# GpSimd tasks of an SSM-plus-SwiGLU kernel wait by semaphore for VectorE's groups of SBUF operations

## The chip, the core and the metric

The kernel runs as one program on 1 core of one Trainium2 chip. The metric is the device time of that core in microseconds. Three runs of the kernel before gave 634.55, 634.59 and 632.18 us, median 634.55 us. Lower is better. The engines are called as the profile calls them: PE is TensorE's matmul, PEld its weight load, DVE is VectorE, ACT is ScalarE, POOL is GpSimd and SP is SyncE, which issues every DMA of this kernel.

## What is computed

The input `x` has 2048 rows of 512 columns. Its rows are normalized, and the result goes down two branches, which are multiplied at the end:

```python
xn = _layernorm(x, axis=-1)
s = _A_ref(xn, A_re, A_im, B_re, B_im, C_re, C_im, log_dt, Dskip)
g = _silu(_B_ref(xn, w_gate, w_up, w_down))
return x + s * g
```

Branch A is a diagonal state-space model. For each of the 512 channels a kernel `K[l] = Re(sum_n C_n * exp(dt*A_n*l) * dt*B_n)` over 128 states is built for 2048 positions, and `xn` is convolved with it by FFTs of length 4096; `xn * Dskip` is added. Branch B is a SwiGLU layer: `(silu(xn @ w_gate) * (xn @ w_up)) @ w_down` with an inner width of 1792.

## The kernel before

**The work.** Branch B is done in float16 pairs: each operand is split into a high and a low half, and three products replace one float32 product. `x` is cut into 8 blocks of 256 rows (index b), the inner width into 7 chunks of 256 columns (index c). A unit (b, c) is 24 matmuls for the gate and 24 for the up side (L708), a silu on ACT (L729), a product on DVE (L731), a cast to the high half on ACT (L733), the low half on DVE (L734), and, some units later, 6 matmuls into the output for each half block (L750). Before that each weight chunk is scaled and split: for `w_up` chunks 1 to 6 POOL multiplies by the scale (L674), ACT casts (L675) and POOL subtracts (L676); for all others ACT scales (L678) and DVE subtracts (L679).

Branch A has four stages. First the parameters are turned into phases and logarithms: DVE does long chains of 128x256 operations whose inputs and outputs all lie in SBUF (L823 to L963: groups of 1 to 11 instructions), with some products on POOL (L821). This is done twice, for two halves of the channels. Second, tables of angles and amplitudes are made on POOL: eight batches of small operations (L1020 to L1061), and from each batch four angle tables (L1079) and four amplitude tables (L1087). For each table ACT takes cosine and sine (L1102 to L1104), DVE multiplies by the amplitudes (L1122 to L1130) and PE multiplies and sums (L1151, 32 small float32 matmuls). Third come the transforms (L572, L1184, L1236, L1243, L1283), with products on DVE (L1261, L1263) and sums on POOL (L1265, L1266). Last, `final` forms the output (L1330 on PE, L1339 on DVE, L1342 on POOL).

**What sets the order.** All this work is entered as tasks in a plan (class `Plan`). A task has an engine, an estimated duration, the buffers it reads and writes, and a due time from the table `W`. `Plan.run` is a list scheduler: it walks through time, starts on each free engine the ready task with the earliest due time, and returns the tasks sorted by their planned start. The program is then written out in that order, one task after the other, so each engine executes its instructions in the planned order, and the tile framework puts semaphore waits where data or a buffer demands them. Planned times have no other effect on the chip: an engine goes on as soon as the data is there. `keep_warm` fills planned gaps of PE with matmuls whose result nobody reads (L1430).

**The port in the plan.** A task can carry the mark `port`. Every POOL task has it, and of the DVE tasks those that were entered with `port=True`: the reciprocal square roots of the layer norm (L535 to L540), the normalization of the rows (L547), the low halves of weights (L679), the scales of `w_down` (L653 to L660), all groups of the parameter stage (L823 to L963 and the exponentials L935 to L952) and the addition of `Dskip` (L1196). In the plan two port tasks never overlap: `start_one` starts each one no earlier than the end of the last:

```python
t.start = max(now, port_free) if t.port else now
...
if t.port:
    port_free = t.end
```

In the program nothing of this is left before the change: if DVE falls behind its planned time, a POOL task that was planned behind a DVE group may run beside it. DVE tasks that take an input from PSUM (L731, L734, L1122 to L1130, L1261, L1263, L1339) do not carry the mark, nor do some very small ones on SBUF (L633).

All working buffers lie in one SBUF tile, `arena`, so most names in the profile read `arena`; the line tells what an instruction is.

Of the kernel before, what the change touches and what calls it, by code (L numbers as in the profile page):

```python
# [46 lines left out]
     "c_akb": 16, "c_gj": 10, "c_kr": 25, "c_y": 42, "c_y2": 16, "c_bh": 6, "c_bt": 14, "c_fx": 15, "c_fz": 2,  # L47
     "c_ot": 24, "c_hh": 15, "c_a": 34, "ah": 384.828, "rs": 4.584, "n1": 14}
REUSE = 0.25
WARM_FROM, WARM_SPAN, WARM_IDLE, WARM_SHARE, WARM_DUR = 1.5, 3.4, 1.0, 0.8, 0.213  # L50
MAGIC = 12582912.0
TWO32 = 4294967296.0
# [23 lines left out]


class Task:
    __slots__ = ("eng", "dur", "fn", "pr", "due", "root", "seq", "deps", "succ", "bufs", "wait", "ready", "dma", "port", "f32", "slack", "ahead", "start", "end")


class Plan:
# [19 lines left out]
    def add(self, eng, dur, fn, rd=(), wr=(), up=(), pr=0.0, c=5, dma=0.0, root=False, port=None, f32=False, slack=0.0, ahead=None):  # L102

        t = Task()
        t.eng, t.dur, t.fn, t.pr, t.due, t.root, t.seq, t.dma = eng, dur, fn, (c, pr), pr, root, len(self.tasks), dma
        t.f32, t.slack, t.ahead = f32, slack, W["ah"] if ahead is None else ahead  # L110
        t.port = eng == "POOL" if port is None else port
        deps = set()
        for b in rd:
            deps.update(b.full)
            deps.update(b.part)
        for b in up:
            deps.update(b.full)
            deps.update(b.reads)
        for b in wr:
            deps.update(b.full)  # L120
            deps.update(b.part)
            deps.update(b.reads)
        for b in rd:
            b.reads.append(t)
        for b in up:
            b.part.append(t)
        for b in wr:
            b.full.append(t)
        t.bufs = list(dict.fromkeys(b for b in (*rd, *wr, *up) if b.kind))
        for b in t.bufs:  # L130
            b.left += 1
        t.deps = deps
        t.succ = []
        self.tasks.append(t)
        return t

    def run(self):
# [14 lines left out]
        ends = []  # L152
        leaving = []
        order = []
# [91 lines left out]
        while left:  # L246
            while leaving and leaving[0][0] <= now + 1e-9:
                give(heapq.heappop(leaving)[3])
            while ends and ends[0][0] <= now + 1e-9:
                _, _, t = heapq.heappop(ends)  # L250
                for b in t.bufs:
                    b.left -= 1
                    if not b.left:
                        heapq.heappush(leaving, (t.end + REUSE, t.seq, b.name, b))
                for s in t.succ:
# [5 lines left out]
            for e in engs:  # L261
                q, h = later[e], heaps[e]
                while q and q[0][0] <= now + 1e-9:
                    _, seq, t = heapq.heappop(q)
# [18 lines left out]
                raise RuntimeError(f"the plan is stuck at {now}: {stuck}, room {room}, banks {banks}")  # L283
            now = min(nxt)
        self.span = max(t.end for t in order)
        order = self.keep_warm(order)
        self.place([b for b in dict.fromkeys(b for t in order for b in t.bufs) if b.kind == "sb"])
        return order

    def keep_warm(self, order):  # L290

        pe = [t for t in order if t.eng == "PE"]
        held = {}
        for t in order:
            for b in t.bufs:
                if b.kind != "sb":
                    o = held.setdefault(b, [t.start, t.end])
                    o[1] = max(o[1], t.end + REUSE)  # L300
        gaps, at = [], WARM_FROM
        for t in pe:
            if t.start - at > 0.3:
                gaps.append((at, t.start))
            at = max(at, t.start + t.dur)
        idle = lambda a: sum(max(0.0, min(e, a + WARM_SPAN) - max(s, a)) for s, e in gaps)
        more = []
        for s, e in gaps:
            if max(idle(a) for a in (s, s - WARM_SPAN / 2, e - WARM_SPAN)) < WARM_IDLE:
                continue  # L310
            free = [(k, i) for k in "ts" for i in range(self.BANKS[k])
                    if not any(b.at == (k, i) and o[0] < e + 0.3 and o[1] > s - 0.3 for b, o in held.items())]
            n = int((e - s - 0.2) * WARM_SHARE / WARM_DUR)
            if n < 1 or not free:
                continue
            for i in range(n):
                t = Task()
                t.eng, t.start, t.dur, t.bufs, t.fn = "PE", s + i * WARM_DUR, WARM_DUR, [], self.warm(free[-1])
                t.end, t.dma, t.deps, t.port, t.f32 = t.start + t.dur, 0.0, set(), False, False
                more.append(t)  # L320
        self.warmed = len(more)
        return sorted(order + more, key=lambda t: t.start)
# [102 lines left out]
def kernel(  # L425
# [7 lines left out]
    nc = tc.nc  # L433
# [45 lines left out]
    bufs = []  # L479
# [18 lines left out]
    def load(dst, src, names, size, pieces, pr, rd=(), ahead=None):  # L498
        add("SP", 0.15, lambda: sy.dma_start(dst(), src), up=names, rd=rd, pr=pr, dma=dma_us(size, pieces), root=True, ahead=ahead)  # L499


    def c_load(name, t, src, pr):
        load(lambda: t, src, [key(name)], 65536, 128, pr)

    add("DVE", 0.2, lambda: (V.memset(ones, 2.0 ** -26), V.memset(halfpi, math.pi / 2)), up=[key("ones")], c=0)
    add("POOL", 0.6, lambda: G.memset(dsk, 0.0), wr=[key("dsk")], c=0)


# [174 lines left out]
    seq = [(b, c) for c in range(NC) for b in range(FB)] + [(b, c) for b in range(FB, NB) for c in range(NC)]  # L683
# [750 lines left out]
    order = pl.run()  # L1434
    for b in bufs:
        b.t = arena if b.kind == "sb" else bank_t[b.at[0]][b.at[1]]
    for t in order:
        t.fn()


# [27 lines left out]
```

## Time and profile before

| | |
|---|---|
| runs of the kernel before | 634.55, 634.59, 632.18 us |
| the profiled execution's own time | 634.03 us |
| span of its profile | 632.3 us |
| mean granted clock of PE over the span | 0.985 |
| PE busy | 606.7 us (96%) |
| DVE busy | 473.3 us (75%) |
| ACT busy | 333.9 us (53%) |
| POOL busy | 331.9 us (52%) |

The span goes from the first instruction to the last; the execution's own time holds 1.7 us more around it. PE is nearly always busy, so what can be gained or lost on it is its idle time and the stretches in which its clock is granted only in part. The stages differ much: DVE is busy 48.6 of the 50 us from 50 to 100 us and 47.5 of the 50 us from 150 to 200 us, but 21.1 of the 50 us from 550 to 600 us. So engines are read in the stage in question and in order of time. In a row of the timeline stand the start in the span, the duration, the engine, the line, the operation, what it writes and reads, the shapes, how many instructions are merged, and in brackets the idle time before it with what ended it.

### The profile page before, as it was taken

How to read it: one execution, taken by the hardware profiler on the slowest of the kernel's cores; microseconds unless marked ns; L12 is line 12 of the kernel's file. 1: busy time of each engine (PE TensorE's matmuls, PEld its weight loads, DVE VectorE, ACT ScalarE, POOL GpSimd, SP SyncE). 2: the span in 40 equal slices, each digit the busy share in tenths (PEclk: the TensorE clock that was granted, in tenths of full speed). 3: DMA queues.
4: the chain of work that ended last, by engine and by line, in shares of the span. 5: the costliest groups of instructions: out<-in, count | busy, mean ns of one | idle time of the engine just before them, and what ended most of it. 6: DMA issues, size and time to landing. Idle time of an engine off the chain costs nothing.

```text
span 632.3 us, 18214 instructions
## 1 busy us (share of the span) xinstructions
PE 606.7 (96%) x7545; PEld 414.8 (66%) x7545; DVE 473.3 (75%) x970; ACT 333.9 (53%) x665; POOL 331.9 (52%) x301
## 2 busy tenths in 40 slices
PE   7989999999979999999999999999999999999894
PEld 3768787576656767776766766766567766557641
DVE  5999999867999897989876967967756566645124
ACT  4977567275635547674877675755642233221100
POOL 0254412798654557767788687976506042431012
PEclk9999999999998999999999999999999999999998
DMA  9985223134000525232313434490396898998997
GB/s 247 356 271 154 81 68 101 35 109 144 18 1 34 108 62 102 92 111 51 82 72 75 116 106 85 69 298 2 118 245 137 279 371 263 257 251 225 227 253 214
DMA packets 134210, 93.06 MB, mean 147 GB/s; under 512 B 72176, under 2 KB 117488, under 8 KB 134128
## 3 DMA queue, kind: packets, MB, share of 16 engines
q1 hardware_dynamic: 134128, 91.90, 52.4%
q8 instruction: 59, 0.97, 0.7%
q14 instruction: 23, 0.19, 0.1%
HBM read 58.98 MB, written 32.90 MB: 145 GB/s over the span
## 4 chain that ended last, share of the span: by engine, by line
PE 44%; DMA 2%; issue 2%; ACT 1%; SPq 1%; DVE 1%; POOL 0%; POOLq 0%; DVEq 0%; ACTq 0%
PE gu L708 20%; PE z L750 10%; PE s L1151 3%; PE s L1236 3%; PE s L1243 2%; PE s L1330 2%; DMA arena<-bs_d 2%; PE s L1283 1%; PE s L1184 1%; PE s L572 1%; DMA out_dram<-arena 1%; DVE arena L1339 0%; SPq L1315 0%; SPq L499 0%; PE t L1283 0%
## 5 line engine op out<-in xcount | busy, mean ns | idle before, releaser
L708 PE MATMUL gu<-arena,wg 128*128 128x256 f16 x1344 | 157.9, 274 | 4.5 <-ACT arena L729 3.8
L750 PE MATMUL z<-wd,arena 128*128 128x512 f16 x672 | 158.6, 380 | 2.0 <-DVE arena L734 1.9
L708 PEld LDWEIGHTS <-wu 128*128 128x128 f16 x1344 | 131.2, 99 | 31.0 <-issue 10.0
L708 PEld LDWEIGHTS <-wg 128*128 128x128 f16 x1344 | 130.9, 98 | 29.2 <-issue 8.4
L708 PE MATMUL gu<-arena,wu 128*128 128x256 f16 x1224 | 144.4, 276 | 5.5 <-DVE arena L734 4.3
L750 PEld LDWEIGHTS <-arena 128*128 128x128 f16 x672 | 61.2, 98 | 82.5 <-issue 14.3
L1087 POOL TENSOR_TENSOR arena<-arena 128x1536 f32<-128x1536 f32 x32 | 91.1, 2851 | 44.5 <-PE s L1151 21.2
L1079 POOL TENSOR_TENSOR arena<-arena 128x1024 int32<-128x1024 int32 x32 | 63.1, 1971 | 27.2 <-ACT t L1104 10.1
L729 ACT ACTIVATE arena<-gu,inv 128x512 f32<-128x512 f32 x56 | 38.5, 687 | 59.4 <-PE gu L708 53.3
L733 ACT CAST arena<-gu 128x512 f16<-128x512 f32 x51 | 29.9, 587 | 64.8 <-DVE gu L731 63.6
L731 DVE SCALAR_TENSOR_TENSOR gu<-gu,shc,arena 128x512 f32<-128x512 f32 x51 | 38.5, 754 | 32.7 <-PE gu L708 32.6
L1102 ACT ACTIVATE t<-arena 128x512 f32<-128x512 int32 x64 | 38.8, 606 | 37.7 <-DVE arena L1124 36.2
L1265 POOL TENSOR_TENSOR arena<-arena 128x512 f32<-128x512 f32 x16 | 20.4, 1275 | 69.3 <-DVE arena L1263 30.7
L1122 DVE TENSOR_TENSOR arena<-arena,t 128x512 f32<-128x512 f32 x64 | 43.6, 681 | 15.6 <-ACT t L1103 7.6
L1342 POOL TENSOR_TENSOR arena<-arena 128x512 f32<-128x512 f32 x12 | 15.2, 1268 | 57.9 <-DVE arena L1339 34.0
L1151 PEld LDWEIGHTS s<-arena 128*32 128x32 f32 x2048 | 31.4, 109 | 19.4 <-issue 13.9
L1103 ACT ACTIVATE t<-t,halfpi 128x512 f32<-128x512 f32 x64 | 42.5, 664 | 1.8
L1104 ACT ACTIVATE t<-arena 128x512 f32<-128x512 int32 x64 | 38.5, 602 | 6.2 <-DVE arena L1263 3.5
L1151 PE MATMUL s<-arena 128*32 128x64 f32 x2048 | 41.3, 222 | 0.0
L734 DVE TENSOR_TENSOR arena<-gu,arena 128x512 f16<-128x512 f32 x51 | 34.8, 682 | 7.2 <-ACT arena L733 7.0
L1339 DVE TENSOR_TENSOR arena<-s,arena 128x512 f32<-128x512 f32 (+1 forms) x20 | 11.3, 581 | 25.6 <-DMA out_dram<-arena 11.7
L1128 DVE SCALAR_TENSOR_TENSOR arena<-arena,t 128x256 f32<-128x256 f32 x64 | 26.4, 412 | 4.1 <-ACT t L1104 4.1
(205 smaller groups left out, 945.3 us busy)
## 6 DMA issues: line engine op xcount, KB each, us to landing
arena<-in_A_u_dram SPq DMA_DIRECT2D x64, 128.0 KB, 3.9
ax_d<-arena SPq DMA_DIRECT2D x32, 256.0 KB, 2.3
ak_d<-arena SPq DMA_DIRECT2D x16, 512.0 KB, 7.4
arena<-ak_d SPq DMA_DIRECT2D x16, 512.0 KB, 7.0
arena<-ax_d SPq DMA_DIRECT2D x16, 512.0 KB, 6.5
bs_d<-arena SPq DMA_DIRECT2D x32, 256.0 KB, 5.1
arena<-in_B_w_down_dram SPq DMA_DIRECT2D x14, 512.0 KB, 5.3
arena<-bs_d SPq DMA_DIRECT2D x14, 512.0 KB, 6.9
```

The costliest lines, as they stand in the source:

```text
L708: T.matmul(pg.t[:, i * 256:(i + 1) * 256].rearrange("p (a t) -> p a t", a=2), w[:, wl, d, i * P:(i + 1) * P], x[:, :, xl, d, :], start=(k ...
L729: add("ACT", 0.69, lambda: S.activation(sg.f32(), pg.t, AF.Silu, scale=inv[:, c, 0:1]), rd=[pg], wr=[sg], c=1, pr=e)
L731: add("DVE", 0.75, lambda: V.scalar_tensor_tensor(pu.t, pu.t, shc[:, c:c + 1], sg.f32(), op0=ALU.mult, op1=ALU.mult), rd=[sg], wr=[pu], c= ...
L734: add("DVE", 0.7, lambda: V.tensor_tensor(hh.view(F16)[:, 512:1024], pu.t, hh.view(F16)[:, 0:512], op=ALU.subtract), rd=[pu], wr=[hh], c=1 ...
L750: T.matmul(z.t, h[:, hl, i * 256 + t * P:i * 256 + (t + 1) * P], w[:, wl, i], start=(c == 0 and i == 0 and k == 0), stop=(c == NC - 1 and ...
L1079: G.tensor_tensor(a, h_[:, :, :, None].to_broadcast([P, 2 * GT, 4, 8]), l_[:, :, None, :].to_broadcast([P, 2 * GT, 4, 8]), op=ALU.add)
L1087: G.tensor_tensor(e, p_[:, :, :, None].to_broadcast([P, 3 * GT, 4, 8]), q_[:, :, None, :].to_broadcast([P, 3 * GT, 4, 8]), op=ALU.mult)
L1102: add("ACT", 0.62, lambda: S.activation(tc_.t, a(), AF.Abs, scale=SIN_SCALE), rd=[an], wr=[tc_], pr=pr)
L1103: add("ACT", 0.7, lambda: S.activation(tc_.t, tc_.t, AF.Sin, bias=halfpi, scale=-1.0), rd=[key("ones")], wr=[tc_], c=4, pr=pr)
L1104: add("ACT", 0.62, lambda: S.activation(ts.t, a(), AF.Sin, scale=SIN_SCALE), rd=[an], wr=[ts], pr=pr + 0.2)
L1122: V.tensor_tensor(o[:, :, 0:64].rearrange("p d (s j) -> p d s j", s=2), e[:, :, 0:64].rearrange("p d (s j) -> p d s j", s=2), t[:, :, None ...
L1151: T.matmul(kt[h * 32:(h + 1) * 32, (r * GD + dd) // 4], o[:, ri, dd + h, 64:96], o[:, ri, dd + h, 0:64], start=(ri == 0), stop=(ri == 1), ...
```

## The change

After the order is fixed, a new pass, `part_ports`, goes through it. For each POOL task it looks at the last DVE port task ahead of it in the order. If that DVE task was planned to start less than 8 us earlier, and no POOL task has been tied to it yet, the POOL task is tied to it. When the program is written, the first instruction of the tied POOL task gets a dependency on the last instruction of the DVE task, which becomes a semaphore wait on POOL. 50 of the 190 POOL tasks are tied. The plan, its order, the buffers and the durations stay as they are. DVE gets no wait for POOL.

```diff
+APART = 8.0
...
     def part_ports(self, order):
+        last = told = None
+        for t in order:
+            if t.port and t.eng == "DVE":
+                last = t
+            elif t.port and t.eng == "POOL" and last is not None and last is not told and t.start - last.start < APART:
+                t.after = told = last
...
         self.span = max(t.end for t in order)
+        self.part_ports(order)
         order = self.keep_warm(order)
...
+    def made():
+        return nc.m.functions[-1].blocks[-1].instructions
+
+    ends = {}
     for t in order:
+        n = len(made())
         t.fn()
+        new = made()[n:]
+        ends[t] = new[-1]
+        if t.after is not None:
+            tc.add_manual_dep(new[0], ends[t.after].name, mybir.DependencyInfo(mybir.DependencyClass.Sync, mybir.DependencyReason.DATA),
+                              reason="ports apart")
```

The instructions of PE, DVE, ACT and SP stand in the same order with the same counts as before; on POOL the order is the same too, and 12 more semaphore instructions stand in it. What differs is what POOL's instructions wait for. In the new file these lines have numbers that are higher by 15 (L821 is L836, L1079 is L1094, L1087 is L1102).

The first place is POOL's part of the early weight stage, from about 28 to 55 us. Before:

```order
L676 TENSOR_TENSOR wu<-wd,wu 128x1024 [waits Activation_49]
L674 TENSOR_TENSOR wd<-wd,scw 128x1024 [waits DMAHW6_49,DVE_49]
L821 TENSOR_TENSOR arena<-arena 128x256 [waits DMAHW7_49,DMAHW4_49]
L821 TENSOR_TENSOR arena<-arena 128x256 [waits DMAHW5_49]
L821 TENSOR_TENSOR arena<-arena 128x256 [waits DMAHW2_49,Pool_49]
```

The same five instructions with the change:

```order
L691 TENSOR_TENSOR wu<-wd,wu 128x1024 [waits DVE_49,Activation_49]
L689 TENSOR_TENSOR wd<-wd,scw 128x1024 [waits DMAHW6_49,DVE_49]
L836 TENSOR_TENSOR arena<-arena 128x256 [waits DMAHW7_49,DMAHW4_49,DVE_49]
L836 TENSOR_TENSOR arena<-arena 128x256 [waits DMAHW5_49]
L836 TENSOR_TENSOR arena<-arena 128x256 [waits DMAHW2_49,Pool_49]
```

The subtraction (L676) gets a wait for DVE's L679, the first product (L821) one for the next L679. The multiplication between them (L674) waited for DVE before too, for its scale; now it waits for a later instruction of DVE, the end of the group L842 to L846.

The second place is POOL's table stage from about 165 to 203 us. Before:

```order
L1087 TENSOR_TENSOR arena<-arena 128x1536 [waits DVE_49,PE_49,Pool_49]
L1079 TENSOR_TENSOR arena<-arena 128x1024 [waits Activation_49]
L821 TENSOR_TENSOR arena<-arena 128x256 [waits DMAHW4_49,DMAHW2_49,Pool_49]
L821 TENSOR_TENSOR arena<-arena 128x256
L821 TENSOR_TENSOR arena<-arena 128x256 [waits Pool_49]
L1087 TENSOR_TENSOR arena<-arena 128x1536 [waits DVE_49,PE_49]
L1079 TENSOR_TENSOR arena<-arena 128x1024
L821 TENSOR_TENSOR arena<-arena 128x256 [waits Pool_49]
L1087 TENSOR_TENSOR arena<-arena 128x1536 [waits DVE_49]
L1079 TENSOR_TENSOR arena<-arena 128x1024 [waits Activation_49]
```

With the change:

```order
L1102 TENSOR_TENSOR arena<-arena 128x1536 [waits PE_49,Pool_49]
L1094 TENSOR_TENSOR arena<-arena 128x1024 [waits DVE_49,Activation_49]
L836 TENSOR_TENSOR arena<-arena 128x256 [waits DMAHW4_49,DMAHW2_49,Pool_49]
L836 TENSOR_TENSOR arena<-arena 128x256
L836 TENSOR_TENSOR arena<-arena 128x256 [waits DVE_49,Pool_49]
L1102 TENSOR_TENSOR arena<-arena 128x1536 [waits PE_49]
L1094 TENSOR_TENSOR arena<-arena 128x1024 [waits DVE_49]
L836 TENSOR_TENSOR arena<-arena 128x256 [waits Pool_49]
L1102 TENSOR_TENSOR arena<-arena 128x1536 [waits DVE_49]
L1094 TENSOR_TENSOR arena<-arena 128x1024 [waits DVE_49,Activation_49]
```

The first amplitude table (L1087) is not tied. The angle table behind it waits for DVE's L825, the third of the three products (L821) for the end of DVE's group L842 to L846, the next angle table (L1079) for the end of the group that begins with L838 and L839 and holds L851 and L852, the last amplitude table for the end of the group L858 to L863, and the last angle table for the end of L935 to L939. The amplitude table in the middle is not tied either; it stands behind the third product. Where a wait for DVE is gone (the first and the middle amplitude table), an earlier wait of POOL on the same semaphore already covers it.

More of the change, by code (lines that the diff above doesn't have):

```diff
@@ L78 @@
 class Task:
-    __slots__ = ("eng", "dur", "fn", "pr", "due", "root", "seq", "deps", "succ", "bufs", "wait", "ready", "dma", "port", "f32", "slack", "ahead", "start", "end")
+    __slots__ = ("eng", "dur", "fn", "pr", "due", "root", "seq", "deps", "succ", "bufs", "wait", "ready", "dma", "port", "f32", "slack", "ahead", "start", "end", "after")
 class Plan:
@@ L109, in add @@
         t.eng, t.dur, t.fn, t.pr, t.due, t.root, t.seq, t.dma = eng, dur, fn, (c, pr), pr, root, len(self.tasks), dma
+        t.after = None
         t.f32, t.slack, t.ahead = f32, slack, W["ah"] if ahead is None else ahead
@@ L288, in run, with part_ports @@
         return order
+    def part_ports(self, order):
+        last = told = None
[4 more added lines that the diff above has]
+                t.after = told = last
     def keep_warm(self, order):
@@ L318, in keep_warm @@
                 t.eng, t.start, t.dur, t.bufs, t.fn = "PE", s + i * WARM_DUR, WARM_DUR, [], self.warm(free[-1])
+                t.after = None
                 t.end, t.dma, t.deps, t.port, t.f32 = t.start + t.dur, 0.0, set(), False, False
```

## Prediction

> **What bounds the kernel now.** I read the page's busy times first, then PE's list of waits, then the timelines of PE, DVE and POOL around the two longest waits.
>
> ```profile
> span 632.3 us, 18214 instructions
> PE 606.7 (96%) x7545; PEld 414.8 (66%) x7545; DVE 473.3 (75%) x970; ACT 333.9 (53%) x665; POOL 331.9 (52%) x301
> PE gu L708 <- ACT arena L729: 4.4, 4, 2.9
> PE gu L708 <- DVE arena L734: 4.3, 1, 4.3
> ```
>
> PE bounds the kernel: it idles 632.3 - 606.7 = 25.6 us. Whatever the change does to POOL and DVE counts only where it moves PE's idle time. The last two rows (waits: total, times, longest) name the largest: one wait of 4.3 us for DVE's L734, and one of 2.9 us for ACT's L729. Here is the first of them, on PE:
>
> ```profile
> 181.49 2.76 PE L750 MATMUL z<-wd,arena 128*128 128x512 f16 x12
> 188.53 5.28 PE L708 MATMUL gu<-arena,wu 128*128 128x256 f16 x24 [4.28 <-DVE arena L734]
> 178.19 2.78 PE L708 MATMUL gu<-arena,wg 128*128 128x256 f16 x24
> 188.50:195.40 6.90, 6.87 (x62) 4.60 (x62) 6.73 (x15) 2.79 (x6) 1.96 (x1) 0.62 0.10 38
> ```
>
> PE is ready at 181.49 + 2.76 = 184.25 and starts at 188.53. After that the same 24 matmuls take 5.28 instead of 2.78 us, and the window from 188.5 to 195.4 has a granted clock of 0.62 (the column behind the five engines). So this stall costs 4.28 + 2.50 = 6.8 us. Why L734 is late stands in DVE's rows, and POOL's beside them:
>
> ```profile
> 166.26 2.04 DVE L825 TENSOR_SCALAR arena<-arena 128x256 f32<-128x256 f32 x1
> 172.79 2.94 DVE L845 TENSOR_TENSOR arena<-arena 128x256 f32<-128x256 f32 x1
> 175.77 1.93 DVE L846 TENSOR_SCALAR arena<-arena 128x256 f32<-128x256 f32 x1
> 180.71 2.89 DVE L839 TENSOR_TENSOR arena<-arena 128x256 f32<-128x256 f32 x1
> 184.55 0.29 DVE L838 TENSOR_SCALAR arena<-arena 128x256 f32<-128x256 f32 x1
> 184.87 0.43 DVE L839 TENSOR_TENSOR arena<-arena 128x256 f32<-128x256 f32 x1
> 187.80 0.68 DVE L734 TENSOR_TENSOR arena<-gu,arena 128x512 f16<-128x512 f32 x1
> 165.32 2.84 POOL L1087 TENSOR_TENSOR arena<-arena 128x1536 f32<-128x1536 f32 x1 [4.87 <-PE s L1151]
> 172.44 3.01 POOL L1087 TENSOR_TENSOR arena<-arena 128x1536 f32<-128x1536 f32 x1
> 175.42 2.13 POOL L1079 TENSOR_TENSOR arena<-arena 128x1024 int32<-128x1024 int32 x1
> 180.48 2.84 POOL L1087 TENSOR_TENSOR arena<-arena 128x1536 f32<-128x1536 f32 x1 [2.19 <-DVE arena L1130]
> ```
>
> The same L839 takes 2.89 us at 180.71 and 0.43 at 184.87. The long one ends at 183.60, just behind the POOL table that ends at 180.48 + 2.84 = 183.32; the next one meets no POOL instruction. L845 ends at 175.73, L1087 at 175.45; L846 at 177.70, L1079 at 177.55. So a DVE instruction on SBUF alone that starts beside a running POOL instruction ends with it, while POOL loses at most 0.17 us (3.01 against 2.84). DVE pays, and the change makes POOL wait.
>
> **The change at this stall.** Free lengths are 0.43 us for a two-input operation and 0.29 for a TENSOR_SCALAR (rows above). The L1087 at 172.44 and the L1079 behind it now run after L846, since the L821 ahead of them is tied to it: L845 and L846 shrink by 2.94 - 0.43 + 1.93 - 0.29 = 4.15 us. The L1087 at 180.48 now waits for the group L858 to L863, so L839 no longer meets it: 2.89 - 0.43 = 2.46 us more. Against that the first L1087 slides: it starts behind L846's new end (177.70 - 4.15 = 173.55) and one L821 (the three at 40.89, below, take 2.63 us together, so 0.9), so it runs from 174.4 to 177.2, and L839 now comes at 180.71 - 4.15 = 176.56: 0.6 us of the 2.46 are lost to it. L734 is then earlier by 4.15 + 2.46 - 0.6 = 6.0 us and ends at 182.5, ahead of PE's 184.25. Even with nothing gained at L839, it ends at 188.48 - 4.15 = 184.33, and the stall is 0.1 us. **I take the whole 6.8 us**; the low end, if the two tables merely meet other instructions of the same groups, is nothing. L825 at 166.26 stays long: the L1087 that it meets is not tied.
>
> **The stall at 46.6 us.**
>
> ```profile
> 40.94 2.78 PE L708 MATMUL gu<-arena,wu 128*128 128x256 f16 x24
> 46.63 4.45 PE L708 MATMUL gu<-arena,wg 128*128 128x256 f16 x24 [2.91 <-ACT arena L729]
> 37.03 2.14 DVE L842 TENSOR_SCALAR arena<-arena 128x256 f32<-128x256 f32 x1
> 39.21 2.00 DVE L843 TENSOR_TENSOR arena<-arena 128x256 f32<-128x256 f32 x1
> 42.97 0.70 DVE L846 TENSOR_SCALAR arena<-arena 128x256 f32<-128x256 f32 x1
> 43.59 0.74 DVE L731 SCALAR_TENSOR_TENSOR z<-z,shc,arena 128x512 f32<-128x512 f32 x1
> 38.98 1.94 POOL L674 TENSOR_TENSOR wd<-wd,scw 128x1024 f32<-128x1024 f32 x1
> 40.89 2.63 POOL L821 TENSOR_TENSOR arena<-arena 128x256 f32<-128x256 f32 x3
> ```
>
> The group L842 to L846 lasts from 37.03 to 43.67, and L731 stands behind it; L731 releases ACT, and ACT releases PE. With L674 held until the group ends, L843 to L846 need 3 x 0.43 + 0.29 and some 0.03 us between them, 1.7 us, from 39.21, so the group ends at 40.9, 2.8 us earlier, which covers the 2.91 us but for 0.1. The matmuls lose 4.45 - 2.78 = 1.67 us to the clock, so this stall costs 4.6 us. How much of it reaches the end is another matter, because later a chain of its own comes in:
>
> ```profile
> 110.67 1.15 ACT L678 ACTIVATE wd<-arena,scw 128x1024 f16<-128x1024 f32 x1
> 113.45 1.41 DVE L679 SCALAR_TENSOR_TENSOR wd<-arena,scw,wd 128x1024 f16<-128x1024 f32 x1
> 115.31 1.46 PE L750 MATMUL z<-wd,arena 128*128 128x512 f16 x6
> 70.62 0.16 PE L624 MATMUL s<-hsq,ones 128*128 128x2 bf16 x1 [0.79 <-DVE hsq L623]
> 79.61 2.78 PE L708 MATMUL gu<-arena,wg 128*128 128x256 f16 x24 [0.92 <-ACT arena L729]
> ```
>
> The last chunk of `w_down` is cast until 111.82, its low half is ready at 114.86, and PE uses it at 115.31, with filler matmuls just ahead. If PE comes there 4.6 us earlier, it waits for this chain. DVE's L679 can follow ACT 113.45 - 111.82 = 1.6 us sooner, no more, unless ACT and the load come sooner too. So the gain here lies between 0 and 4.6 us, or 6.3 with the two small waits at 70.62 and 79.61 us, in a stretch in which DVE is as late. **I take 1.5 us**, by this 1.6.
>
> **What the waits cost.** Behind a waiting POOL instruction stand the tables, and for those wait ACT's L1102, DVE's L1122 and, through them, PE's L1151. The tightest place I found:
>
> ```profile
> 221.57 2.11 POOL L1079 TENSOR_TENSOR arena<-arena 128x1024 int32<-128x1024 int32 x1 [7.14 <-DVE arena L946]
> 227.56 1.75 DVE L883 RECIPROCAL arena<-arena 128x256 f32<-128x256 f32 x1
> 228.98 0.62 ACT L1102 ACTIVATE t<-arena 128x512 f32<-128x512 int32 x1
> 229.63 0.66 ACT L1103 ACTIVATE t<-t,halfpi 128x512 f32<-128x512 f32 x1
> 233.58 0.69 DVE L1122 TENSOR_TENSOR arena<-arena,t 128x512 f32<-128x512 f32 x1 [0.88 <-PE s L803]
> ```
>
> This angle table is tied to the group that ends with L883 at 229.31. It then ends at 231.4 instead of 223.68, and ACT's L1102 starts 2.4 us late. Its cosine follows 1.3 us after its start (L1103 ends at 230.29), at 232.7, still ahead of DVE's 233.58. So DVE covers it; uncovered it would be 2.4 us. The other end is nothing. I take 0.5 us. 12 more semaphore instructions on POOL stand on no path to PE.
>
> **Sum.** 632.3 - 6.8 - 1.5 + 0.5 = 624.5 us of span. Around the span lie 634.03 - 632.3 = 1.7 us: 626.2 us for the profiled execution, which was 0.5 us below the median of the runs. So **626.7 us** for the median, 1.2% less.
>
> TensorE: Matmul & The Clock Gate, section Part 1: The HAM clock gate, of the Trainium skill, says that the clock falls to half after an idle window of about 3.4 us. The 4.28 us stall fits this; the 2.91 us stall with its 4.45 us matmuls is shorter than that and lost clock all the same. By that rule the early stall would be priced at 2.9 instead of 4.6 us, and the sum would stay as it is, since only 1.5 of it is counted.
>
> **Rivals.** *A rest of the clash stays.* POOL is ordered behind DVE, but DVE is not ordered behind POOL: the untied L1087 slides by 2 us, as worked out above, and may meet more of the next group. For it speaks L825 (166.26), which stays long. If half of the 4.28 us remains as a stall with clock loss in proportion, the first term is 3.4 us instead of 6.8: 626.7 + 3.4 = 630.1 us. Against it: L734 has 1.8 us to spare by the working. The Trainium skill (SBUF — State Buffer, section Who interferes with whom) says that whichever of the two starts first holds the shared ports for its whole instruction and the other blocks; that is this rival's mechanism, and the rows of L839 agree as far as POOL comes first.
>
> *The gain goes into a later limit.* The end is dense with transfers:
>
> ```profile
> 608.00:616.00 8.00, 7.59 (x39) 3.52 (x40) 0.00 (x0) 0.26 (x1) 0.00 (x0) 1.00 1.06 244
> 440.00:448.00 8.00, 8.00 (x91) 6.02 (x89) 6.20 (x14) 4.70 (x8) 8.00 (x6) 1.00 0.01 2
> SPq L1199 <- DVE arena L1196: 15.9, 2, 10.4
> ```
>
> From 608 to 616 us the transfers' share (the last column but one) is over 1 and DVE does nothing. If this were a bound of its own, little would be gained: 633.5 us. Against it: from 440 to 448 us the share is 0.01, and the transfers behind that wait for DVE's L1196 (10.4 us at a time), so their start moves with the compute.
>
> *Slower: the tables come late.* If DVE's groups do not get shorter, each tied POOL task waits out its group in full. The place is the table at 221.57: it comes 2.4 us too late for ACT. ACT executes in order, so the silu and the cast for PE stand behind; PE stalls 2.4 us, and at the ratio of the early stall (1.67 / 2.91) loses 1.4 us of clock. With both old stalls left this is 634.55 + 3.8 = 638.4 us. It decides from the point where a table's delay exceeds its reader's reserve: here 7.7 against 228.98 - 223.68 = 5.3 us. Against it: L839's two lengths.
>
> *The waits do nothing,* because DVE is done before POOL comes: 634.5 us. Against it, the rows of 180.48 and 38.98: the one starts before the group L858 to L863, which stands behind L734 at 187.80, the other before L846's end at 43.67.
>
> **How the numbers follow.** Forecast 0.60, rest of the clash 0.18, later limit 0.10, tables late 0.07, waits without effect 0.05. About 0.5% is what a measurement of this kernel can tell: below 631.4 us is faster, above 637.7 slower. Forecast and first rival are faster: 0.78. Later limit and no effect are the same: 0.15. Tables late: 0.07. Downwards the range reaches the whole early gain, 6.3 instead of 1.5 us: 626.7 - 4.8 = 621.9. Upwards it takes in the first rival and stops at 633.0, ahead of the later limit; what is left out is about 0.2.
>
> **What would show it.** Right: no PE wait above 1 us between 50 and 590 us, a granted clock of 1.0 around 185 us; L845, L846 and L839 in this stage below 1.2 us; L825 still near 2; the L1087 after the L821 starting behind L846; PE's L750 on the last `w_down` chunk still at 112 to 115 us. Wrong: PE waiting for L1151's inputs or for ACT's L729 between 215 and 300 us, L1102 waiting for POOL's L1079 there, or DVE's groups as long as before.

## The result and the profile after

The changed kernel takes 618.92 us (median of four runs, 618.50 to 620.62) against 634.57 us for the kernel before, timed beside it: the ratio is 0.976, with a 95% interval of 0.972 to 0.980. A second series gave 619.64 us and 0.979 (0.976 to 0.982). The change gains 2.1 to 2.4%, between 13 and 16 us. The forecast was 626.7 us with a range from 621.9 to 633.0 us: right in its sign, but only about half of the gain, and the time lies 3 us below the range.

The page of the changed kernel and PE's list of waits there (total, times, longest). In it L708 is L723, L734 is L749, L750 is L765 and L839 is L854.

```profile
span 616.7 us, 18226 instructions
PE 599.4 (97%) x7545; PEld 411.9 (67%) x7545; DVE 444.4 (72%) x970; ACT 335.0 (54%) x665; POOL 327.9 (53%) x301
PE z L765 <- DVE arena L749: 2.1, 1, 2.1
PE gu L723 <- ACT arena L744: 0.5, 2, 0.3
```

DVE is busy 28.9 us less with the same 970 instructions, POOL 4.0 us less. PE idles 17.3 us in place of 25.6, and it is busy 7.3 us less, 4.2 of which are the lost clock behind the two stalls (1.67 + 2.50). Both waits that bounded the kernel before are gone: L723 now waits 0.5 us in all for ACT's silu (L744), and no longer at all for DVE's L749.

PE's timeline in the changed kernel around the two places and near the end (start and duration of the groups of matmuls), then the row of the kernel before that answers to the last one, and the changed kernel's window from 184 to 191 us, in which the column behind the five engines is the granted clock:

```profile
39.98 2.78 PE L723 MATMUL gu<-arena,wu 128*128 128x256 f16 x24
42.65 2.78 PE L723 MATMUL gu<-arena,wg 128*128 128x256 f16 x24
...
174.51 2.76 PE L765 MATMUL z<-wd,arena 128*128 128x512 f16 x12
177.11 2.78 PE L723 MATMUL gu<-arena,wu 128*128 128x256 f16 x24
...
577.90 0.59 PE L765 MATMUL z<-wd,arena 128*128 128x512 f16 x2
```

```profile
593.07 0.59 PE L750 MATMUL z<-wd,arena 128*128 128x512 f16 x2
```

```profile
184.00:191.00 7.00, 7.00 (x99) 4.85 (x104) 6.32 (x18) 5.43 (x16) 1.92 (x2) 1.00 0.10 37
```

Neither group waits, and both run at full clock. The same instructions in the two kernels give **PE's lead**, the measure used from here on. At the 24 matmuls of 39.98 us it is 40.94 - 39.98 = 0.96 us. This part is not the change's: ahead of the first clash the lead differs from trace to trace, from -0.9 to +1.9 us in the kernels below, so each lead is read together with its start. At the 12 matmuls ahead of the late stall it is 181.49 - 174.51 = 6.98 us, so the early part gave 6.0 us. At the next 24 matmuls it is 188.53 - 177.11 = 11.42, and as they take 2.78 in place of 5.28 us, 13.92 behind them: the late stall gave 6.9 us. Near 578 us, at the two L750 that start at 593.07 us in the kernel before, it is 15.17.

DVE's and POOL's timelines at the late stall, changed kernel:

```profile
159.28 2.05 DVE L840 TENSOR_SCALAR arena<-arena 128x256 f32<-128x256 f32 x1
165.63 0.42 DVE L860 TENSOR_TENSOR arena<-arena 128x256 f32<-128x256 f32 x1
166.09 0.29 DVE L861 TENSOR_SCALAR arena<-arena 128x256 f32<-128x256 f32 x1
169.01 1.20 DVE L853 TENSOR_SCALAR arena<-arena 128x256 f32<-128x256 f32 x1
170.31 0.43 DVE L854 TENSOR_TENSOR arena<-arena 128x256 f32<-128x256 f32 x1
174.94 0.68 DVE L749 TENSOR_TENSOR arena<-gu,arena 128x512 f16<-128x512 f32 x1
166.53 0.73 POOL L836 TENSOR_TENSOR arena<-arena 128x256 f32<-128x256 f32 x1 [1.68 <-DVE arena L861]
```

L860 and L861 (L845 and L846 before) fell from 2.94 and 1.93 to 0.42 and 0.29 us; the tied L836, with the tables queued behind it, waits for L861. L840, which meets an untied table, still takes 2.05 us.

### The profile page after: what moved, and what is told of

The parts are those of the page before. It is cut to its first block, busy times and chain, and to the rows that moved or that the text cites. A ratio compares the mean times of both kernels' runs of the same rounds, so it can differ in the third digit from the quotient of the medians.

```text
span 616.7 us, 18226 instructions
## 1 busy us (share of the span) xinstructions
PE 599.4 (97%) x7545; PEld 411.9 (67%) x7545; DVE 444.4 (72%) x970; ACT 335.0 (54%) x665; POOL 327.9 (53%) x301
## 4 chain that ended last, share of the span: by engine, by line
PE 85%; DMA 6%; DVE 4%; SPq 2%; ACT 2%; issue 1%; DVEq 0%
PE gu L723 41%; PE z L765 21%; PE s L1166 6%; DMA arena<-bs_d 3%; PE s L1251 3%; PE s L587 2%; DMA arena<-zg_d 2%; PE s L1258 2%; PE z L723 2%; PE s L1345 2%; PE s L1298 1%; PE s L1199 1%; DMA arena<-in_A_u_dram 1%; PE s L570 1%; SPq L530 1%
## 5 line engine op out<-in xcount | busy, mean ns | idle before, releaser
L765 PE MATMUL z<-wd,arena 128*128 128x512 f16 x672 | 158.5, 380 | 2.2 <-DVE arena L749 2.1
L723 PE MATMUL gu<-arena,wg 128*128 128x256 f16 x1344 | 156.3, 273 | 1.0 <-ACT arena L1205 0.7
L723 PEld LDWEIGHTS <-wu 128*128 128x128 f16 x1344 | 130.8, 98 | 26.1 <-issue 5.3
L723 PEld LDWEIGHTS <-wg 128*128 128x128 f16 x1344 | 130.0, 98 | 24.8 <-issue 5.6
L723 PE MATMUL gu<-arena,wu 128*128 128x256 f16 x1224 | 143.6, 275 | 1.2 <-ACT arena L1205 0.7
L765 PEld LDWEIGHTS <-arena 128*128 128x128 f16 x672 | 61.2, 98 | 81.9 <-issue 13.5
L1102 POOL TENSOR_TENSOR arena<-arena 128x1536 f32<-128x1536 f32 x32 | 91.1, 2851 | 25.5 <-PE s L1166 12.3
L1094 POOL TENSOR_TENSOR arena<-arena 128x1024 int32<-128x1024 int32 x32 | 62.8, 1963 | 30.1 <-ACT arena L1205 9.9
L744 ACT ACTIVATE arena<-gu,inv 128x512 f32<-128x512 f32 x56 | 38.6, 689 | 58.1 <-PE gu L723 53.9
L749 DVE TENSOR_TENSOR arena<-gu,arena 128x512 f16<-128x512 f32 x51 | 34.8, 683 | 7.6 <-ACT arena L748 7.5
L1268 ACT COPY arena<-s 128x512 f32<-128x512 f32 x28 | 15.5, 589 | 25.0 <-PE t L1251 13.2
```

The costliest lines, as they stand in the source:

```text
L723: T.matmul(pg.t[:, i * 256:(i + 1) * 256].rearrange("p (a t) -> p a t", a=2), w[:, wl, d, i * P:(i + 1) * P], x[:, :, xl, d, :], start=(k ...
L744: add("ACT", 0.69, lambda: S.activation(sg.f32(), pg.t, AF.Silu, scale=inv[:, c, 0:1]), rd=[pg], wr=[sg], c=1, pr=e)
L749: add("DVE", 0.7, lambda: V.tensor_tensor(hh.view(F16)[:, 512:1024], pu.t, hh.view(F16)[:, 0:512], op=ALU.subtract), rd=[pu], wr=[hh], c=1 ...
L765: T.matmul(z.t, h[:, hl, i * 256 + t * P:i * 256 + (t + 1) * P], w[:, wl, i], start=(c == 0 and i == 0 and k == 0), stop=(c == NC - 1 and ...
L1094: G.tensor_tensor(a, h_[:, :, :, None].to_broadcast([P, 2 * GT, 4, 8]), l_[:, :, None, :].to_broadcast([P, 2 * GT, 4, 8]), op=ALU.add)
L1102: G.tensor_tensor(e, p_[:, :, :, None].to_broadcast([P, 3 * GT, 4, 8]), q_[:, :, None, :].to_broadcast([P, 3 * GT, 4, 8]), op=ALU.mult)
```

## The experiments

Each time stands beside runs of the kernel before on the same chip. The first five kernels carry only a part of the ties; they differ from the changed kernel in one condition of `part_ports`.

**The ties before 100 us alone**

```diff
-            elif t.port and t.eng == "POOL" and last is not None and last is not told and t.start - last.start < APART:
+            elif t.port and t.eng == "POOL" and last is not None and last is not told and t.start - last.start < APART and t.start < 100.0:
```

> Only the POOL tasks that the plan starts before 100 us are tied; the later ones run as before. Theory (two independent stalls, the early gain reaches the end whole): PE gains 6 to 7 us by 84 us as with the whole change, keeps it to 164 us, then meets the old stall for L734 at about 177 us with 4.3 us and the clock loss behind it; time 628 us, 1.0% below before. Rival (the prediction's step: the chain of the last w_down chunk gives the early gain back unless the later waits help DVE too): PE waits between 100 and 120 us, and the time is 632.5 us or more.

Measured: 627.77 us, ratio 0.991 (0.989 to 0.993). PE's lead, at the same two places as above:

```profile
174.51 2.76 PE L765 MATMUL z<-wd,arena 128*128 128x512 f16 x12
181.58 4.45 PE L723 MATMUL gu<-arena,wu 128*128 128x256 f16 x24 [4.30 <-DVE arena L749]
586.43 0.59 PE L765 MATMUL z<-wd,arena 128*128 128x512 f16 x2
```

The lead is 6.98 us at the first row, 1.40 us of which stood before 40 us already, and 593.07 - 586.43 = 6.64 us at the last. The late stall stands as it was (4.30 us). Between 100 and 120 us PE waits once, 0.41 us at 110.58 for ACT's L772, and not for the chunk. So nearly all of the early gain passes the last chunk of `w_down` and reaches the end, without any help from the later ties. The prediction had counted 1.5 us of it.

**The ties behind 100 us alone**

```diff
+            elif ... and t.start - last.start < APART and t.start >= 100.0:
```

> Only the POOL tasks that the plan starts at 100 us or later are tied. Theory: the stall at 46.6 us is there as before (2.9 us and slow matmuls behind it), the one at 188.5 us is gone, and 7 to 8 us reach the end; time 626.5 us, 1.2% below before, and the two parts add up to the whole change's 15.6 us. Rival (the stall at 188.5 us also needs the early waits, because DVE comes there late from the early stage): a stall of 1 us or more is left at 184 to 189 us and the time is 629 us or more.

Measured: 626.56 us, ratio 0.989 (0.987 to 0.991).

```profile
181.52 2.76 PE L765 MATMUL z<-wd,arena 128*128 128x512 f16 x12
184.12 2.78 PE L723 MATMUL gu<-arena,wu 128*128 128x256 f16 x24
585.00 0.59 PE L765 MATMUL z<-wd,arena 128*128 128x512 f16 x2
```

There is no lead ahead of the stall, it is 188.53 - 184.12 + 2.50 = 6.9 us behind it, and 8.07 us at the end. The two halves add up: 0.9% and 1.1% make 2.0%, against 2.1 to 2.4% for the whole change; in the traces, whose starts differ, 6.64 + 8.07 = 14.71 us against 15.17.

**Four ties, and one**

```diff
+TIED = (39.31, 169.14, 174.75, 180.83)
...
+            elif ... and any(abs(t.start - s) < 0.01 for s in TIED):
```

> Four of the 50 waits alone: the early L674 for the group L842 to L846, and in the table stage the third L821 for L842 to L846, the L1079 behind it for the group with L851 and L852, the next L1087 for L858 to L863. Theory (four clashes make both large stalls): both stalls gone or below 0.5 us, some small waits at 64 to 80 us stay; time 622 to 624 us, three quarters of the change's gain. Rival (many small clashes make the gain together): half of it or less, 627 us or more.

Measured: 625.82 us, ratio 0.988 (0.985 to 0.991), between the two expectations. PE at the late place (lines shifted by one more):

```profile
178.23 2.76 PE L766 MATMUL z<-wd,arena 128*128 128x512 f16 x12
180.83 2.78 PE L724 MATMUL gu<-arena,wu 128*128 128x256 f16 x24
```

The lead ahead of the late stall is 181.49 - 178.23 = 3.3 us, behind it 188.53 - 180.83 + 2.50 = 10.2: the three late ties gave the whole 6.9 us. Of the 3.3 us ahead of it 1.92 stood before 40 us already, so the early tie gave only 1.3 us of the 6.0 that the early part gave with all ties. With that one alone:

```diff
+            elif ... and abs(t.start - 39.31) < 0.01:
```

> One wait alone: the early L674 for the group L842 to L846. Theory: PE's stall at 46.6 us is gone (4.6 us gained at 50 us), but the groups behind it (L838 to L863, L951) stay long, so DVE is late again by 70 to 80 us and PE waits there; 2 to 4.6 us reach the end, time 630 to 632.5 us. Rival (the early gain is that one stall alone): 4.7 us reach the end undiminished, time 629.8 us, and PE has no wait over 1 us between 50 and 120 us.

Measured: 631.29 us, ratio 0.996 (0.995 to 0.998). The time is where the theory put it, and for its reason, but the gain is lost near 57 us and not at 70 to 80. The timelines of PE, DVE and POOL in the kernel with one tie:

```profile
43.72 2.78 PE L723 MATMUL gu<-arena,wg 128*128 128x256 f16 x24 [0.88 <-ACT arena L744]
57.78 0.16 PE L639 MATMUL s<-hsq,ones 128*128 128x2 bf16 x1 [1.97 <-ACT arena L826]
179.49 2.76 PE L765 MATMUL z<-wd,arena 128*128 128x512 f16 x12
46.24 2.24 DVE L866 SCALAR_TENSOR_TENSOR arena<-arena 128x256 f32<-128x256 f32 x1
50.76 1.95 DVE L873 TENSOR_SCALAR arena<-arena 128x256 f32<-128x256 f32 x1
45.88 2.31 POOL L691 TENSOR_TENSOR wu<-wd,wu 128x1024 f16<-128x1024 f32 x1
50.67 1.89 POOL L689 TENSOR_TENSOR wd<-wd,scw 128x1024 f32<-128x1024 f32 x1 [2.48 <-DVE scw L648]
```

The tie does its work: the wait of 2.91 us becomes 0.88, and the matmuls behind it keep full clock. But at 57.78 us stands a new wait of 1.97 us, because DVE's L866 and L873 are now held by the two untied POOL instructions of 45.88 and 50.67 us. The lead is 181.49 - 179.49 = 2.0 us, 0.88 of which stood before 40 us. So the gain of this tie was not stopped at `w_down`, at 115 us, but at once, by the next untied neighbours. To see the neighbours by themselves, a kernel got three early ties, the one of before and those on these two instructions:

```diff
+TIED = (39.31, 46.60, 51.29)
```

> The kernel before with three ties alone: the GpSimd tasks planned at 39.31 us (L689, the one tied alone before), 46.60 us (L691) and 51.29 us (L689). With the first alone, TensorE led by 4.6 us at 56 us and lost 2.6 of it behind a wait of 1.97 us at 57.78 us; there VectorE's L866, L873 and L854 stood beside the two others. Theory (those two untied instructions took the gain back): the wait near 57 us goes, TensorE is 5 to 6.5 us ahead from 84 us to the end, 628 to 629.5 us. Rival (the loss near 57 us has another cause, as the later start of GpSimd's first task): 2 us ahead at 84 us as with one tie, 631 to 632.5 us.

Measured: 630.68 us, ratio 0.997 (0.995 to 0.998), which is neither of the two expectations in full. DVE's and PE's timelines in it (lines shifted by one more):

```profile
57.48 2.10 DVE L952 TENSOR_SCALAR arena<-arena 128x256 f32<-128x256 f32 x1
62.76 1.47 PE L724 MATMUL gu<-arena,wg 128*128 128x256 f16 x12 [1.40 <-ACT arena L745]
178.25 2.76 PE L766 MATMUL z<-wd,arena 128*128 128x512 f16 x12
```

The wait near 57 us is gone, and the same thing happens one step later: L952 (L951 in the changed kernel) meets the next untied POOL instruction, and PE waits 1.40 us at 62.76. The lead is 181.49 - 178.25 = 3.2 us, 0.32 of which stood before 40 us. In the traces, without what stood before, one tie gave 1.1 us, three 2.9 and all early ones 6.0: each passes on what the ones before it gained. The times alone do not tell one tie from three (2.1 and 2.4 us below the kernel before).

**The ties the other way round**

```diff
-            if t.port and t.eng == "DVE":
+            if t.port and t.eng == "POOL":
                 last = t
-            elif t.port and t.eng == "POOL" and last is not None and ...
+            elif t.port and t.eng == "DVE" and last is not None and ...
```

> The same ties the other way round: a VectorE task on SBUF waits for the end of the GpSimd task that the plan has started last, and GpSimd waits for no VectorE task. Theory (VectorE is held to the end of the GpSimd instruction beside which it starts, so a wait for that end costs what the holding cost): no gain, 632 to 638 us, and the stalls of TensorE near 47 and 188 us stay above 2 us each. Rival (the gain comes from the two engines never using SBUF side by side, whoever waits): 619 to 625 us.

Measured: 636.81 us, ratio 1.005 (1.003 to 1.007), half a per cent slower. PE waits 3.68 us at 47.97 us, and at the late place:

```profile
191.81 4.34 PE L723 MATMUL gu<-arena,wu 128*128 128x256 f16 x24 [4.84 <-DVE arena L749]
```

DVE's timeline at the two places:

```profile
40.12 1.97 DVE L857 TENSOR_SCALAR arena<-arena 128x256 f32<-128x256 f32 x1 [1.95 <-POOL wu L691]
183.98 2.88 DVE L854 TENSOR_TENSOR arena<-arena 128x256 f32<-128x256 f32 x1
```

As the theory has it, nothing is gained. But ties in this direction do not part the engines. POOL has no wait for DVE's groups, so its next instruction starts beside the DVE group that has just waited for the last one: L857 waits 1.95 us for POOL's L691 and is then held for 1.97 us by L689, which started at 40.04, and L854 takes 2.88 us beside a table that started at 183.75. DVE pays with the wait and with the hold. So waits on DVE alone gain nothing here; whether parting the engines in full would pay whoever waits, as the rival has it, stays open.

**GpSimd waits for any VectorE task**

```diff
-            if t.port and t.eng == "DVE":
+            if t.eng == "DVE":
                 last = t
```

> As the change, but GpSimd waits for the VectorE task last planned before its own, of any kind, also those that read PSUM, which makes the waits later by one or two VectorE instructions at 124 places. Theory (the waits cost GpSimd time that its reserves cover): within 2 us of the changed kernel, 618 to 621 us. Rival (the tables of L1094 and L1102, which in the changed kernel end 0.03 to 0.07 us before their use, come late): 623 us or more, with TensorE or VectorE waiting for L1094 between 190 and 300 us.

Measured: 620.68 us, ratio 0.978 (0.976 to 0.980), as the theory has it. Although waits moved to a later instruction at 124 places, PE gained only one wait behind 100 us, of 0.66 us for L749 at 186.57.

**Shorter GpSimd instructions, without ties**

```diff
-            G.tensor_tensor(a, h_[:, :, :, None].to_broadcast([P, 2 * GT, 4, 8]),
-                            l_[:, :, None, :].to_broadcast([P, 2 * GT, 4, 8]), op=ALU.add)
+            for q in (slice(0, GT), slice(GT, 2 * GT)):
+                G.tensor_tensor(a[:, q], h_[:, q, :, None].to_broadcast([P, GT, 4, 8]),
+                                l_[:, q, None, :].to_broadcast([P, GT, 4, 8]), op=ALU.add)
```

The amplitude tables are cut in three in the same way.

> The kernel before, no ties, with each GpSimd instruction of L1079 cut in two and each of L1087 in three of about 1 us. Theory (a VectorE instruction on SBUF ends with the one GpSimd instruction beside which it starts): the VectorE instructions in the groups around 170 to 187 us take at most 1.5 us in place of 2 to 2.9, TensorE's stall near 188 us falls from 4.28 to below 2 us and its slow 24 matmuls behind it (5.28) to 2.8, the stall near 47 stays, and the time is 627 to 631 us. Rival (VectorE is held for as long as GpSimd has work ready, whatever its pieces): stall as before, 632 to 636 us.

Measured: 633.46 us, ratio 0.999 (0.997 to 1.000): no change to speak of, though around 170 to 187 us the kernel did what the theory says.

The timelines of DVE, PE and POOL:

```profile
171.87 0.83 DVE L845 TENSOR_TENSOR arena<-arena 128x256 f32<-128x256 f32 x1
185.72 2.78 PE L708 MATMUL gu<-arena,wu 128*128 128x256 f16 x24 [1.92 <-DVE arena L734]
...
398.87 4.63 DVE L1198 TENSOR_TENSOR arena<-arena,dsk 128x64 f32<-128x64 f32 x1
407.94 1.08 PE L1153 MATMUL s<-arena 128*32 128x64 f32 x32 [3.21 <-DVE arena L1170]
398.17 2.10 POOL L1080 TENSOR_TENSOR arena<-arena 128x512 int32<-128x512 int32 x2
400.22 3.13 POOL L1089 TENSOR_TENSOR arena<-arena 128x512 f32<-128x512 f32 x3
```

L845 takes 0.83 in place of 2.94 us, the stall near 188 us falls from 4.28 to 1.92 us, and the matmuls behind it keep full clock. But at 398.87 us a single 128x64 instruction of DVE is held for 4.63 us, across the rest of one piece of POOL and four more, until 403.50, just behind the last (400.22 + 3.13 = 403.35). PE then waits 3.21 us at 407.94, its next matmuls are slow, and the gain is gone: its lead falls from 4.1 us to -0.6 us there. The Trainium skill (SBUF — State Buffer, section Who interferes with whom) says that whichever engine issues first holds the shared ports for its whole instruction and blocks the other; the many DVE instructions of this trace that end with one POOL instruction agree, this one was held past four boundaries between instructions.

**The chain over the last chunk of `w_down`, made longer**

```diff
-        t.fn()
+        for _ in range(4 if t.eng == "ACT" and abs(t.start - 104.393) < 0.01 else 1):
+            t.fn()
```

> The changed kernel with the ScalarE instruction L693 on the last chunk of w_down (103.69 us there) run four times in place of once, so that VectorE's L694 and TensorE's L765 get that chunk 3 times 1.06 = 3.2 us later. Theory (the chain over the last chunk of w_down does set TensorE there, with a reserve of 2.2 us in the changed kernel): TensorE waits 1.0 us at L765 near 108 us or loses it to later instructions, and all behind it runs 1.0 to 1.5 us later to the end. Rival 1 (it has no reserve worth the name): 3 us later. Rival 2 (TensorE does not depend on it within 5 us): no change, below 0.3 us.

Measured: 621.07 us (two runs). The timelines of ACT and PE:

```profile
104.36 4.69 ACT L693 ACTIVATE wd<-arena,scw 128x1024 f16<-128x1024 f32 x4
110.43 1.24 PE L765 MATMUL z<-wd,arena 128*128 128x512 f16 x5 [0.94 <-DVE wd L694]
179.30 2.78 PE L723 MATMUL gu<-arena,wu 128*128 128x256 f16 x24
```

This trace runs 0.67 us later than the changed kernel's ahead of the place (L693 at 104.36, there 103.69) and 2.19 us later behind it (179.30, there 177.11). PE waits 0.94 us for DVE's L694, and of 3.55 us more on the chain (4.69 in place of 1.14) it loses 1.5. The chain does limit PE, as the prediction said, with a reserve of about 2 us in the changed kernel.

**Two instructions in another order near 580 us, and fewer fillers**

```diff
+    i = next(i for i, t in enumerate(order) if t.eng == "DVE" and abs(t.start - 580.25) < 0.01)
+    k = next(i for i, t in enumerate(order) if t.eng == "DVE" and abs(t.start - 581.16) < 0.01)
+    order.insert(k, order.pop(i))
```

> The changed kernel with two VectorE instructions near 580 us the other way round: L749, for which TensorE waits 2.12 us at 580.62, ahead of L1354, which waits 4.11 us for the load of arena<-zg_d. Theory (TensorE still sets the end): the wait goes, and so do the slow matmuls behind it (7.07 us for 48, in place of 5.40), 2.1 to 3.8 us in all, 615 to 617 us. Rival (at the end the transfers set the time, as the DMA engines are busy 0.9 and more of their time from 570 us on): TensorE waits as much later at L1345 for arena<-bs_d or for L1354, 618 to 620 us.

```diff
-            if n < 1 or not free:
+            if n < 1 or not free or s > 30.0:
```

> The same swap, and without the filler matmuls (L1445) that the plan puts in behind 30 us: 7 of them at 107.25 to 109.63 us and 3 at 412.70. Theory (TensorE comes early enough now that some of them only take its time): 0.8 us less at 107 us, where L765 could start 2.2 us sooner, and 0.6 us less at 412.70, so 1 to 1.5 us less than with the swap alone. Rival (TensorE waits there in any case): within 0.4 us of the swap alone.

> The changed kernel again, beside the two above on the same chip. 618 to 620.6 us as before; its tail behind 575 us and its first 20 us may differ by 1 us from run to run.

Measured side by side: 619.83 us with the swap, 619.54 us with both, 619.64 us for the changed kernel, whose ranges all overlap. PE's timeline with the swap alone:

```profile
592.69 1.08 PE L1345 MATMUL s<-arena,j_t 128*64 128x256 f32 x8 [1.64 <-DMA arena<-bs_d]
604.95 5.38 PE L1345 MATMUL s<-arena,j_t 128*64 128x256 f32 x20 [3.29 <-DVE arena L1354]
```

and the same instruction as in the last row in the changed kernel's second trace:

```profile
606.21 2.81 PE L1345 MATMUL s<-arena,j_t 128*64 128x256 f32 x20 [3.17 <-DVE arena L1354]
```

The wait at L765 is gone with the swap, and PE waits 1.64 us for a load at 592.69 and 3.29 us for L1354 at 604.95. L1354 in its turn waits for the transfers into and out of its buffers. In the changed kernel's second trace the wait at L765 is 0.70 in place of 2.12 us without any swap, and the time is no shorter. So in the last 30 us the transfers set the time, as the rival said. Without the fillers PE gains some 0.6 us at each of the two places, by the starts of the same matmuls ahead of them and behind them, and that too is gone at the end. None of these versions beats the changed kernel.

## Why the prediction was right or wrong

**The mechanism** held. The DVE instructions grew short exactly where POOL was tied (L860, L861, L854), and L840 beside an untied table stayed at 2.05 us.

**The late stall** was sized right: 6.8 us forecast, 6.9 measured, and 6.9 again with the late ties alone. That the two agree to 0.1 us is partly luck, since 2.50 of it is lost clock, and behind a stall of the same length other traces lost less (last section). L853 and L854 took 0.9 us from the sliding table where 0.6 was worked out (1.20 in place of 0.29 us at 169.01), and L749 ended at 175.62, 1.65 us ahead of PE's 177.27, where 1.75 was worked out.

**The early stall** is the step that failed. The prediction found its 4.6 us, and 6.3 with the two waits behind it, and then counted 1.5 us, since "DVE's L679 can follow ACT 113.45 - 111.82 = 1.6 us sooner, no more, unless ACT and the load come sooner too". They did come sooner. ACT's timeline at the chunk before the last and ahead of the last one in the kernel before, and then ACT, DVE and PE in the changed one:

```profile
105.07 1.15 ACT L678 ACTIVATE wd<-arena,scw 128x1024 f16<-128x1024 f32 x1 [1.50 <-DMA arena<-in_B_w_down_dram]
107.76 0.69 ACT L729 ACTIVATE arena<-gu,inv 128x512 f32<-128x512 f32 x1 [1.06 <-issue]
```

```profile
97.79 1.15 ACT L693 ACTIVATE wd<-arena,scw 128x1024 f16<-128x1024 f32 x1 [1.09 <-DMA arena<-in_B_w_down_dram]
100.78 0.69 ACT L744 ACTIVATE arena<-gu,inv 128x512 f32<-128x512 f32 x1 [0.88 <-PE gu L723]
...
103.69 1.14 ACT L693 ACTIVATE wd<-arena,scw 128x1024 f16<-128x1024 f32 x1
104.87 1.29 DVE L694 SCALAR_TENSOR_TENSOR wd<-arena,scw,wd 128x1024 f16<-128x1024 f32 x1
108.33 1.46 PE L765 MATMUL z<-wd,arena 128*128 128x512 f16 x6
```

The cast of the last chunk waited for no transfer. It stood in ACT's queue behind the silu (L729) and a row of small operations, with no idle time between them, and the silu follows PE's own gate matmuls, as the changed kernel's row names them. So the chain rides on PE: it started 110.67 - 103.69 = 6.98 us earlier, exactly PE's lead, and DVE, no longer in its clash, followed at once and left PE 108.33 - 106.16 = 2.2 us of reserve in place of 115.31 - 114.86 = 0.45. The loads came sooner as well: the chunk before the last does wait for its transfer, in both kernels, and is cast 105.07 - 97.79 = 7.28 us earlier, for SP, which issues these loads, waits in its turn for DVE's L679 (11.5 us in three waits between 60 and 112 us in the kernel before). A start time in the trace of before had been taken for a fixed one. The row that would have told was the one ahead of it in ACT's queue, and the mark set for this, L750 at 112 to 115 us, came out at 108.33. The early part gave 6.0 us, which is 4.5 more than the term.

**The cost of the waits** was taken as 0.5 us and is nothing that shows. The place was well chosen: the table is late there, and ACT waits 2.01 us for it, where 2.4 was worked out. It was also named as a sign of being wrong (L1102 waiting for L1079 between 215 and 300 us); it came, and it cost PE nothing. After:

```profile
215.16 1.96 POOL L1094 TENSOR_TENSOR arena<-arena 128x1024 int32<-128x1024 int32 x1 [9.91 <-ACT arena L1205]
217.15 0.60 ACT L1117 ACTIVATE t<-arena 128x512 f32<-128x512 int32 x1 [2.01 <-POOL arena L1094]
```

The first row names ACT's L1205, which ended last ahead of it, but in the kernel before the same table ran 6 us ahead of that instruction; the wait is the tie, as DVE's L898 ends at 213.28 + 1.75 = 215.03. DVE covers it, PE has no wait above 0.34 us from 199 to 320 us, and with later waits at 124 places the time moved by less than 2 us.

**What remains** of the difference between the spans, 624.5 forecast and 616.7 measured: 7.8 us are 4.5 of the early term, 0.1 of the late one and 0.5 of the waits; 1.0 us that PE led before 40 us already; and 1.2 us gained in small steps near 306 and 424 us; the rest lies in the last 30 us. The lead before 40 us is not the change's: the kernel with shorter tables, which has no ties and the same instructions up to there, led the trace of before by 1.0 us as well. The step near 424 us stands also in the trace with the ties reversed.

**The rivals.** None of them set the time. No rest of the clash held PE at the late place, the table that came late for ACT did not come late for PE, and the gain went into the end's transfers only in the last 30 us, where the wait for L765 (1.90 us before, 2.12 after) had no bearing on the time. This wait is also the one exception to the mark of no wait above 1 us between 50 and 590 us. The range reached down to 621.9 us by counting the whole early gain of 6.3 us; it left no room for the start, for the small steps and for waits at no cost.

## What to carry to other kernels

Before a gain is written off against a later chain, follow that chain back in its engine's queue: if it ends at the bounding engine itself, with no idle time between, it moves along and limits only beyond its reserve, here about 2 us. A link that waits for a transfer is not fixed for that alone: ask what the transfer's issue waits for. Where two engines hold each other up, let the one give way that has reserve, here GpSimd; waits laid on VectorE instead left the holds standing and lost 0.5%. Ties of this kind work as a set, and a single one is judged too low, since the next untied clash takes its gain.

## What the runs showed of the hardware

A DVE instruction of 128x64 elements was held for 4.63 us across five consecutive POOL instructions, while in the same trace others ended with the one beside which they had started; shorter pieces on POOL that stand back to back do not always bound the hold. Small instructions are held as well: DVE's L648 on 128x2 elements took 1.91 us at 28.94 us in the changed kernel and ended at 30.85, beside a POOL instruction that ended at 30.83. And POOL is held where DVE comes first, so that the prediction's "POOL loses at most 0.17 us" holds for its own rows only: in the kernel before, POOL's L1051 took 1.36 us at 113.74, beside DVE's L679 (113.45 to 114.86), and 0.38 us at its fastest.

The length of a stall does not alone decide what it costs in clock: behind 3.17 us of idle time PE kept full clock (2.81 us for 20 L1345 at 606.21), behind 2.91 us at 46.63 before it lost 1.67 us, and behind nearly equal stalls of 4.28 to 4.30 us the same 24 matmuls took 5.28 us in two traces, 5.03 and 4.45 in two others.
